# Reading the streamed operand of a matmul as two halves in turn, and the columns of all weight blocks 8 bytes apart

## Chip, cores and metric

The kernel runs on one core of a Trainium2 chip. The metric is the time of one execution on the device in microseconds (us). Before the change the median of three runs is 941.89 us, the lowest 941.58 us and the highest 941.97 us.

## What is computed

The reference is attention in a causal window of 128 positions with a linear bias per head, followed by a feed-forward block with a squared ReLU. There are 8 batches of 576 positions (4608 tokens), 8 heads of 64, a model width of 512 and a hidden width of 2048, all in float32.

```python
scores = scale * np.matmul(q, k.transpose(0, 1, 3, 2))
mask = (rel >= 0) & (rel < window)            # window = 128
scores = np.where(mask, scores + bias[None], -1000000000.0)
attn = np.exp(scores - np.max(scores, axis=-1, keepdims=True))
attn = attn / (np.sum(attn, axis=-1, keepdims=True) + 1e-09)
x = np.matmul(attn, v)                        # as (4608, 512)
h = np.maximum(x @ w_in, 0.0)                 # w_in (512, 2048)
return h * h @ w_out                          # w_out (2048, 512)
```

## The kernel before

**Tiling.** The 4608 tokens are cut into 9 chunks of 512 (`NCH`), the hidden width into 16 blocks of 128 (`NF`), the model width into 4 blocks of 128 (`NCC`). Everything in the feed-forward part is kept transposed: features lie on the 128 partitions, the 512 tokens of a chunk along each partition.

**The two products.** For each chunk `c` and hidden block `f`, `gemm1` (L194) makes one 128x512 result out of twelve matmuls (L202): four blocks `cc` of the model width, three matmuls each. `gemm2` (L223) adds to four 128x512 accumulators `acc`, one for each block `m` of the output, with three matmuls each (L231), twelve again. So each product has 9 x 16 x 12 = 1728 matmuls of 512 columns. Three matmuls stand for one float32 product: weight and data are each split into a high and a low part in a float32 type that TensorE takes in one pass (`F32R`, shown as fp32r or f32), and high times high, high times low and low times high are added. The streamed operands are `xs[cc][:, part]` (tile `xu`, part 0 high and part 1 low) in `gemm1`, and `hh` and `hl` in `gemm2`. Each is a row of 512 consecutive 4-byte words on every partition. Each matmul is recorded as two instructions: a weight load (LDWEIGHTS, engine PEld) of 128 columns, and the matmul itself (MATMUL, engine PE).

**Weights.** All weights stay in the on-chip memory. `weights_load` brings them in as pairs of 32-bit words (the inputs are float64, reinterpreted), and `convert` turns each pair in place into a low and a high part. So `self.w[f]` has the shape 128 x 2 x 512 x 2: product, column, low or high. `block` (L185) gives `gemm1` and `gemm2` the 128 columns of a block. Their words stand 8 bytes apart, since low and high alternate. For the blocks that `APART` (L39) picks, the host has stored the columns of two neighbouring blocks alternating, and `block` takes every second one, so that the words of one block stand 16 bytes apart. `APART` picks the first product alone, `f` = 0, 4, 8, 12, and of its four blocks the first two: six of the twelve weight loads of every fourth `gemm1`.

**Order.** TensorE's order is written out by hand. From chunk 1 on, the loop in `tile_attn_moe` alternates `gemm1` of step `n` with `gemm2` of step `n - 2`; once in eight such halves a `visit` puts the small matmuls of the attention (L541, L548) between them. Chunk 0 is ordered by a small planner with costs and due times (`Plan`, `start`), together with loads, weight conversion and the attention of the first chunks. Between the two products ScalarE and VectorE make `hh` and `hl` out of the result (L212 to L221). At the end of each chunk the four accumulators are copied out and written to the output, transposed; the host transposes it back.

Of the kernel before, what the change touches and what calls it, by code (L numbers as in the profile page):

```python
# [19 lines left out]
B, H, S, D = 8, 8, 576, 64  # L20
NP = H // 2
DM, DF = 512, 2048
NF = DF // 128
NCC = DM // 128
NCH = B * S // 512
# [10 lines left out]
GO = 20  # L36
SOON = (("z", 7),)
FIRST = 39
APART = lambda i, f, b: i == 0 and f % 4 == 0 and b < 2  # L39
CASTS = (0, 2, 15,)  # L40
COPIES = (3,)
SQUARES = (6,)
# [14 lines left out]

def slope(h):
    return 2.0 ** (-8.0 * (h + 1) / H)


class Kern:
# [120 lines left out]


    def block(self, i, f, b):  # L185

        w = self.w[f][:, i]
        if APART(i, f, b):
            w = w.rearrange("p (n j o) t -> p n o j t", n=2, o=2)[:, b // 2, b % 2]
        else:  # L190
            w = w[:, 128 * b : 128 * b + 128]
        return w[..., 0], w[..., 1]

    def gemm1(self, c, f):  # L194
        nc = self.nc
        xs = [self.x[c, p] for p in range(NP)]
        g = self.big.tile([128, 2, 512], F32, name="g")[:, 1] if self.big else self.g1.tile([128, 512], F32, name="g")
        i = 0
        for cc in range(NCC):
            wl, wh = self.block(0, f, cc)  # L200
            for w, part in ((wh, 0), (wh, 1), (wl, 0)):
                nc.tensor.matmul(g, w, xs[cc][:, part], start=i == 0, stop=i == 11)  # L202
                i += 1
                if (c, f, i) == (0, 0, 9):
                    yield
        yield
        r = self.hp.tile([128, 512], F32, name="r", bufs=1)
        hh = self.hp.tile([128, 512], F32R, name="hh")
        hl = self.hp.tile([128, 512], F32R, name="hl")
        self.h[c, f] = hh, hl  # L210
        with self.tc.high_priority(offset=100):
            self.relu = nc.scalar.activation(r, g, AF.Relu)  # L212
        yield
        if c or f in SQUARES:
            nc.vector.tensor_tensor(r, r, r, op=ALU.mult)  # L215
        else:
            nc.scalar.activation(r, r, AF.Square)
        yield
        nc.scalar.copy(hh, r)  # L219
        yield  # L220
        nc.vector.tensor_tensor(hl, r, hh.bitcast(F32), op=ALU.subtract)  # L221

    def gemm2(self, c, f):  # L223
        nc = self.nc
        hh, hl = self.h.pop((c, f))
        if f == 0:
            self.acc = self.start_banks if c == 0 else [self.ac.tile([128, 512], F32, name="acc") for _ in range(4)]
        for m in range(4):
            wl, wh = self.block(1, f, m)
            for i, (w, h) in enumerate(((wh, hh), (wh, hl), (wl, hh))):  # L230
                nc.tensor.matmul(  # L231
                    self.acc[m], w, h, start=(f == 0 and i == 0), stop=(f == NF - 1 and i == 2)
                )
            if f == NF - 1:
                o = self.op.tile([128, 512], F32, name="o")
                out = self.outd[m * 128 : m * 128 + 128, 512 * c : 512 * c + 512]
                (nc.scalar.copy if m % 2 else nc.vector.tensor_copy)(o, self.acc[m])
                (nc.scalar if c == NCH - 1 and m == 3 else nc.sync).dma_start(out, o)
# [598 lines left out]
def _consts():  # L837
    r = np.arange(128)
    own, h = r % 64, (r // 64)[:, None]
    cst = np.zeros((128, CST), np.float32)  # L840
    cst[:, 0:128] = np.eye(128)
    keep = own[:, None] >= np.arange(64)[None, :]
    cst[:, 128:192] = np.where(h == 0, keep, ~keep).astype(np.int32).view(np.float32)
    cst[:, 192:256] = NEG
    rel = r[:, None] - r[None, :]
    rel = np.where(rel >= 0, rel, rel + 128)
    for a in range(H):
        cst[:, 256 + 128 * a : 384 + 128 * a] = -rel * (8 * slope(a))
    later = r[:, None] < r[None, :]
    near = [cst[:, 256 + 128 * a : 384 + 128 * a] for a in range(H)]  # L850
    return np.concatenate([cst] + [np.where(late, t, np.float32(NEG)) for t in near for late in (later, ~later)], axis=1)


def _arrays(q, k, v, moe_w_in, moe_w_out):
    a = np.ascontiguousarray
    pairs = lambda x: x.transpose(1, 3, 0, 2).reshape(NP, 128, B * S)
    halo = lambda x: np.concatenate([np.zeros((NP, 128, 128), np.float32), x], axis=2)
    qt, kt = pairs(q), halo(pairs(k))
    qkd = np.stack([np.concatenate([
        qt[:, :, 512 * c : 512 * c + 256], kt[:, :, 512 * c : 512 * c + 640], qt[:, :, 512 * c + 256 : 512 * c + 512],  # L860
    ], axis=2) for c in range(NCH)])
    vt = np.zeros((NP, 1 + B * S // 128, 128, 128), np.float32)
    vt[:, 1:] = v.reshape(B, NP, 2, S, D).transpose(1, 0, 3, 2, 4).reshape(NP, B * S // 128, 128, 128)
    vd = np.stack([vt[:, 4 * c : 4 * c + 5].transpose(0, 2, 1, 3).reshape(NP, 128, 640) for c in range(NCH)])
    w1d = a(moe_w_in.reshape(NCC, 128, NF, 128).transpose(2, 1, 0, 3).reshape(NF, 128, NCC * 128))
    w2d = moe_w_out.reshape(NF, 128, DM).copy()
    for i, w in enumerate((w1d, w2d)):
        for f in range(NF):
            for n in range(2):
                if APART(i, f, 2 * n):  # L870
                    x = w[f, :, 256 * n : 256 * n + 256]
                    x[:] = x.reshape(128, 2, 128).transpose(0, 2, 1).reshape(128, 256).copy()
    return [a(qkd), a(vd), w1d.view(np.int64), w2d.view(np.int64), _consts()]


# [16 lines left out]
```

## Time and profile before

| what | value |
|---|---|
| median of three runs | 941.89 us |
| span of the profiled execution, first to last instruction | 939.1 us |
| L202 (first product), PE busy in the span | 423.89 us, 1728 matmuls |
| L231 (second product), PE busy in the span | 424.92 us, 1728 matmuls |
| PE busy, 0 to 35 us | 31.82 us |
| PE busy, 35 to 150 us | 112.80 of 115.00 us |
| PE busy, 300 to 700 us | 400.00 of 400.00 us |
| PE busy, 860 to 939.1 us | 75.38 of 79.10 us |

The profile was taken of one execution. Its page gives the span, from the first to the last instruction, and no separate device time for that execution; the device times of the three runs lie 2.5 to 2.9 us above the span. Records of matmuls overlap, since one starts streaming before the one ahead of it has drained; so the mean length of a record is no pace, and the pace is read from the distance between starts. PE is TensorE's matmuls, PEld its weight loads, which run beside them; DVE is VectorE, ACT is ScalarE.

### The profile page before, as it was taken

What the parts mean: (1) busy time and instruction counts of PE and PEld (TensorE: products, weight loads), DVE (VectorE), ACT (ScalarE), POOL (GpSimd) and SP (SyncE); (2) the same over time, 40 slices, a digit from 0 to 9 for tenths busy, and PEclk for the clock granted to TensorE, in tenths of its full rate; (3) what the DMA queues carried; (4) which work ended last, traced back from release to release, by engine and by line L of the source; (5) the groups of instructions that cost most, each with busy time, mean ns of one, the idle gap of its engine ahead of it and who ended that gap; (6) DMA issues with size and microseconds to landing.
All of it is one profiled execution on the core that took longest, in us unless ns stands there. A gap on an engine that the chain in (4) does not pass through costs nothing.

```text
span 939.1 us, 19485 instructions
## 1 busy us (share of the span) xinstructions
PE 929.3 (99%) x7492; PEld 782.5 (83%) x7492; DVE 497.2 (53%) x1326; ACT 418.9 (45%) x1115; POOL 214.2 (23%) x255
## 2 busy tenths in 40 slices
PE   8899999999999999999999999999999999999998
PEld 5688888888888888888888888888888888888886
DVE  5999874445554555544555444455455454433222
ACT  7898753343444444334434343344444444322222
POOL 4223331222221222222222222221221222220000
PEclk9999999999999999999999999999999999999999
DMA  9975424222432233222423233334322231111001
GB/s 344 403 284 167 135 74 130 71 62 83 129 86 85 78 104 107 64 84 79 125 86 86 73 106 82 86 85 127 88 77 83 75 93 43 38 46 45 1 0 45
DMA packets 72893, 95.26 MB, mean 101 GB/s; under 512 B 8032, under 2 KB 41952, under 8 KB 72800
## 3 DMA queue, kind: packets, MB, share of 16 engines
q1 hardware_dynamic: 72368, 93.36, 32.6%
q8 instruction: 59, 0.97, 0.4%
q10 hardware_dynamic: 432, 0.66, 0.2%
q14 instruction: 34, 0.28, 0.1%
HBM read 67.76 MB, written 26.21 MB: 100 GB/s over the span
## 4 chain that ended last, share of the span: by engine, by line
PE 94%; DMA 3%; DVE 1%; ACT 1%; issue 0%; SPq 0%; POOLq 0%; DVEq 0%
PE acc L231 43%; PE g L202 42%; PE s L541 5%; PE g L548 2%; DMA raw<-in_dram 2%; PE s L548 1%; DMA wide<-in_dram 1%; PE at L346 1%; ACT t L470 0%; PE s L412 0%; PE at L412 0%; DVE t L482 0%; DVE tw L613 0%; DVE pp L629 0%; DVE raw L175 0%
## 5 line engine op out<-in xcount | busy, mean ns | idle before, releaser
L202 PE MATMUL g<-xu,w 128*128 128x512 f32 x1728 | 423.9, 394 | 1.4 <-issue 0.8
L202 PEld LDWEIGHTS g<-xu,w 128*128 128x128 f32 x1728 | 344.6, 209 | 56.7 <-issue 1.7
L231 PE MATMUL acc<-hh,w 128*128 128x512 f32 x1152 | 385.6, 396 | 0.0
L231 PEld LDWEIGHTS acc<-hh,w 128*128 128x128 f32 x1152 | 224.0, 194 | 45.5 <-issue 5.3
L212 ACT ACTIVATE r<-g 128x512 f32<-128x512 f32 x144 | 86.1, 598 | 353.2 <-PE g L202 353.1
L215 DVE TENSOR_TENSOR r<-r 128x512 f32<-128x512 f32 x129 | 91.9, 713 | 255.8 <-ACT r L212 255.8
L231 PE MATMUL acc<-hl,w 128*128 128x512 f32 x576 | 226.2, 393 | 0.0
L334 POOL TENSOR_SCALAR_AFFINE_SELECT pp<-pp 128x512 f32<-128x512 f32 x128 | 112.5, 879 | 215.6 <-DMA pp<-way 139.4
L221 DVE TENSOR_TENSOR hl<-r,hh 128x512 fp32r<-128x512 f32 x144 | 117.6, 816 | 74.4 <-ACT hh L219 71.9
L270 POOL TENSOR_TENSOR t<-t,nm 128x512 f32<-128x512 f32 x64 | 76.1, 1190 | 262.0 <-DVE nm L267 231.4
L231 PEld LDWEIGHTS acc<-hl,w 128*128 128x128 f32 x576 | 112.1, 195 | 19.6
L219 ACT CAST hh<-r 128x512 fp32r<-128x512 f32 x144 | 89.2, 619 | 78.0 <-DVE r L215 76.4
L259 ACT ACTIVATE t<-t,nm 128x128 f32<-128x128 f32 x256 | 100.1, 394 | 11.8 <-DVE nm L252 11.7
L321 DVE STREAM_TRANSPOSE pp<-t 128x512 f32<-128x512 f32 x64 | 45.2, 707 | 47.0 <-POOL t L270 39.5
L252 DVE CUSTOM_DVE_ANT_0 t<-t,cst 128x128 f32<-128x128 f32 x256 | 59.5, 295 | 1.0
L541 PE MATMUL s<-pp,v 64*64 64x128 f32 (+1 forms) x1792 | 52.0, 248 | 0.1
L541 PEld LDWEIGHTS s<-pp,v 64*64 64x64 f32 x1792 | 40.5, 134 | 10.4 <-issue 10.0
L259 ACT ACTIVATION_READ_ACCUMULATOR t<-t,nm 128x1 f32 x256 | 48.6, 190 | 0.0
L482 DVE COPY_PREDICATED t<-cst,s 64x256 f32<-64x256 int32 x100 | 44.4, 444 | 6.0 <-ACT t L463 3.1
L472 POOL MEMSET t<- 64x128 f32 (+1 forms) x44 | 10.0, 228 | 117.8 <-PE s L548 110.5
L529 ACT CAST xu<-s 128x512 fp32r<-128x512 f32 x28 | 16.4, 587 | 41.6 <-DVE t L482 26.6
L470 ACT COPY t<-g 64x256 f32<-64x256 f32 (+2 forms) x86 | 28.0, 340 | 3.8 <-PE g L548 1.0
(71 smaller groups left out, 482.3 us busy)
## 6 DMA issues: line engine op xcount, KB each, us to landing
raw<-in_dram SPq DMA_DIRECT2D x32, 512.0 KB, 8.7
way<-pp SPq DMA_DIRECT2D x256, 64.0 KB, 2.0
pp<-way SPq DMA_DIRECT2D x64, 256.0 KB, 2.8
qk<-in_dram SPq DMA_DIRECT2D x32, 320.0 KB, 3.2
v<-in_dram SPq DMA_DIRECT2D x32, 320.0 KB, 3.9
qk<-in_dram SPq DMA_DIRECT2D x38, 256.0 KB, 4.3
out_dram<-o SPq DMA_DIRECT2D x35, 256.0 KB, 2.6
v<-in_dram SPq DMA_DIRECT2D x3, 256.0 KB, 5.2
```

The costliest lines, as they stand in the source:

```text
L202: nc.tensor.matmul(g, w, xs[cc][:, part], start=i == 0, stop=i == 11)
L212: self.relu = nc.scalar.activation(r, g, AF.Relu)
L215: nc.vector.tensor_tensor(r, r, r, op=ALU.mult)
L219: nc.scalar.copy(hh, r)
L221: nc.vector.tensor_tensor(hl, r, hh.bitcast(F32), op=ALU.subtract)
L231: nc.tensor.matmul(self.acc[m], w, h, start=(f == 0 and i == 0), stop=(f == NF - 1 and i == 2))
L252: self.nc.vector.tensor_tensor_reduce(self.t[:, m], self.t[:, m], self.K.nrel(2 * self.p + m // 2), -0.125, BIG, ALU.add, ALU.min, self.nm ...
L259: return self.nc.scalar.activation(self.t[:, m], self.t[:, m], AF.Exp, bias=nm[:, m : m + 1], scale=-1.0, accum_out=nm[:, 4 + m : 5 + m],)
L270: self.nc.gpsimd.tensor_tensor(self.t, self.t, self.nm[:, 8:12].unsqueeze(2).to_broadcast([128, 4, 128]), op=ALU.mult)
L321: nc.vector.transpose(squares.rearrange("p b m c -> p m b c"), self.t.rearrange("p m (b c) -> p m b c", c=32))
L334: nc.gpsimd.affine_select(to, self.own, pattern=[[-32 * sign, 4], [0, 4], [-sign, 32]], compare_op=op, fill=0.0, base=0, channel_multiplie ...
L541: made.append(mm(to, w, x, start=first and n < 2, stop=not first, skip_group_check=True))
```

## The change

The moving operand of all 3456 matmuls of the two products is read in another order. `in_turn` views a row of 512 words as two halves of 256 and runs over them in turn: word 0, word 256, word 1, word 257 and so on. Neighbouring words of the stream are then 1024 bytes apart, and the words of each half follow one another at every second place. The number of words, and the set of words, is as before.

`APART` is gone. Every weight block is 128 neighbouring columns, with words 8 bytes apart; the host stores the weights without the alternation.

As the stream's order sets the order of the result's columns, each product permutes the 512 tokens of a chunk once; the host puts them back with two permutations of the output.

Both edits change addresses alone: on every engine and queue the same instructions stand in the same order, with the same shapes.

```diff
-APART = lambda i, f, b: i == 0 and f % 4 == 0 and b < 2
...
+def in_turn(x):
+    return x.rearrange("p (a b) -> p b a", a=2)
...
     def block(self, i, f, b):
-
-        w = self.w[f][:, i]
-        if APART(i, f, b):
-            w = w.rearrange("p (n j o) t -> p n o j t", n=2, o=2)[:, b // 2, b % 2]
-        else:
-            w = w[:, 128 * b : 128 * b + 128]
+        w = self.w[f][:, i, 128 * b : 128 * b + 128]
         return w[..., 0], w[..., 1]
...
-                nc.tensor.matmul(g, w, xs[cc][:, part], start=i == 0, stop=i == 11)
+                nc.tensor.matmul(g, w, in_turn(xs[cc][:, part]), start=i == 0, stop=i == 11)
...
-                    self.acc[m], w, h, start=(f == 0 and i == 0), stop=(f == NF - 1 and i == 2)
+                    self.acc[m], w, in_turn(h), start=(f == 0 and i == 0), stop=(f == NF - 1 and i == 2)
...
-    w2d = moe_w_out.reshape(NF, 128, DM).copy()
-    for i, w in enumerate((w1d, w2d)):
-        for f in range(NF):
-            for n in range(2):
-                if APART(i, f, 2 * n):
-                    x = w[f, :, 256 * n : 256 * n + 256]
-                    x[:] = x.reshape(128, 2, 128).transpose(0, 2, 1).reshape(128, 256).copy()
-    return [a(qkd), a(vd), w1d.view(np.int64), w2d.view(np.int64), _consts()]
+    w2d = moe_w_out.reshape(NF, 128, DM)
+    return [a(qkd), a(vd), w1d.view(np.int64), a(w2d).view(np.int64), _consts()]
...
-    return np.ascontiguousarray(r.results[0]["out_0_dram"].T)
+    out = r.results[0]["out_0_dram"].T
+    for _ in range(2):
+        out = out.reshape(NCH, 256, 2, DM).transpose(0, 2, 1, 3).reshape(B * S, DM)
+    return np.ascontiguousarray(out)
```

## The prediction, made before the changed kernel ran

> **What bounds the kernel now.** I read the page's totals first, then its chain, then the groups of instructions, then TensorE's waits.
>
> ```profile
> span 939.1 us, 19485 instructions
> PE 929.3 (99%) x7492; PEld 782.5 (83%) x7492; DVE 497.2 (53%) x1326; ACT 418.9 (45%) x1115; POOL 214.2 (23%) x255
> PEclk9999999999999999999999999999999999999999
> PE acc L231 43%; PE g L202 42%; PE s L541 5%; PE g L548 2%; DMA raw<-in_dram 2%; PE s L548 1%; DMA wide<-in_dram 1%; PE at L346 1%; ACT t L470 0%; PE s L412 0%; PE at L412 0%; DVE t L482 0%; DVE tw L613 0%; DVE pp L629 0%; DVE raw L175 0%
> L202 PE MATMUL g<-xu,w 128*128 128x512 f32 x1728 | 423.9, 394 | 1.4 <-issue 0.8
> L231 PE MATMUL acc<-hh,w 128*128 128x512 f32 x1152 | 385.6, 396 | 0.0
> L231 PE MATMUL acc<-hl,w 128*128 128x512 f32 x576 | 226.2, 393 | 0.0
> ```
>
> TensorE is busy for 99% of the span, at the full granted clock in every slice. The chain that ended last runs through the two products for 43% and 42% of the span. They are 1728 + 1152 + 576 = 3456 matmuls of 512 columns, and before the first product TensorE waits 1.4 us in all. So each nanosecond that the change puts on a matmul's pace, or takes off it, counts 3456 times, and there is next to no slack that could swallow it. All other engines are busy half of the span or less.
>
> **The pace of a matmul now.** Records overlap, so I take it from a run of twelve on the timeline (start, length, and the count). The first row is a `gemm1` whose `f` is a multiple of 4, so with six weight loads at 16 bytes; the second is one without.
>
> ```profile
> 289.44 2.97 PE L202 MATMUL g<-xu,w 128*128 128x512 f32 x12
> 300.52 2.92 PE L202 MATMUL g<-xu,w 128*128 128x512 f32 x12
> 14.00 0.59 PE L129 MATMUL g<-zero 128*128 128x512 bf16 x2
> L129 PE MATMUL g<-zero 128*128 128x512 bf16 x2 | 0.6, 379 | 0.0
> ```
>
> Twelve matmuls have eleven distances and one last record of 0.39 us (the mean of 394 ns above). Without `APART` that is (2.92 - 0.39) / 11 = 0.230 us per matmul. With it the run is 2.97 - 2.92 = 0.05 us longer, 6 x 8 ns. The third and fourth rows show a stream of equally many columns, but 2-byte words, at full clock: 0.59 - 0.379 = 0.21 us from start to start, with the row's rounding up to 0.216. The 4-byte stream is thus 14 to 19 ns slower per 512 columns, although it has as many columns. Something that goes with bytes seems to hold it.
>
> **What a read costs by its step.** The change's own operation, a stream whose neighbouring words are far apart, stands nowhere in the trace: every matmul there streams consecutive words, or pieces of at least 32 of them. The nearest rows are weight loads, which read the same memory 128 words at a time with three steps. The first row is six loads at 16 bytes (in a window from 289.15 to 290.55 us), the second six at 8 bytes (from 300.25 to 301.6 us), the third loads of consecutive words in the attention, the fourth the same with 64 columns, the last all loads of the first product.
>
> ```profile
> L202 PEld LDWEIGHTS g<-xu,w 128*128 128x128 f32 x6 | 1.5, 309 | 0.0
> L202 PEld LDWEIGHTS g<-xu,w 128*128 128x128 f32 x6 | 1.2, 194 | 0.2
> L581 PEld LDWEIGHTS s<-qk 64*128 64x128 f32 x24 | 1.6, 186 | 2.5 <-DVE nm L591 1.6 <-DMA qk<-in_dram 0.9
> L541 PEld LDWEIGHTS s<-pp,v 64*64 64x64 f32 x1792 | 40.5, 134 | 10.4 <-issue 10.0
> L202 PEld LDWEIGHTS g<-xu,w 128*128 128x128 f32 x1728 | 344.6, 209 | 56.7 <-issue 1.7
> ```
>
> Sixty-four more columns of consecutive words cost 186 - 134 = 52 ns, so 128 columns take 104. From consecutive words to a step of 8 bytes the load grows by 8 ns, from 8 to 16 bytes by 115 ns. That fits a memory that hands out pieces of 16 bytes (my reading of the rows): 32, 64 and 128 pieces for the three loads, where the first is held by its columns (104 ns) and the others by their pieces. The price of a piece is then (309 - 194) / (128 - 64) = 1.80 ns. The stream of 512 consecutive 4-byte words takes 128 pieces, and 128 x 1.80 = 230 ns, which is just its measured pace; the 2-byte stream takes 64 pieces, 115 ns, and is held by its columns at 0.21 us instead. I take this agreement of two unlike operations as the strongest hint of the trace: the streams of the two products already run at the pace at which pieces arrive.
>
> **The change part by part.**
>
> *`APART` removed.* Six matmuls in every fourth `gemm1` lose about 8 ns each. There are 9 x 4 = 36 such runs: 36 x 0.05 = 1.8 us, and with a distance of 45 ns instead of the rounded 50 it is 1.6 us. All of it lies on TensorE's path. I take -1.6 us. If streams become much slower than loads, the loads at 16 bytes would have been hidden anyway and this gain is part of the rest; it never costs.
>
> *The streams in turn.* The cost per matmul lies between two ends. The lower end: a reader that keeps the piece of each half until its four words are used fetches 128 pieces as before, 0 ns; it could even lose the hold and come down to the 2-byte row's pace, about -14 to -19 ns. The upper end: a reader that fetches anew whenever the next word lies in another piece fetches 512 pieces, 512 x 1.80 = 920 ns per matmul, 690 ns more. The row nearest to the new stream is the weight load at 16 bytes, for it alone uses one word of a piece and goes on to another, and it pays the full 1.80 ns each time. It is not quite the same, since there the rest of the piece is never wanted, and here it is wanted two words later. I take the upper end: nothing in the trace shows that a reader holds more than the piece that it is on, and the price has been seen in two kinds of rows. So 3456 x 690 = 2385 us.
>
> What covers this? Nothing: TensorE is the engine that all wait for. The work of DVE, ACT and POOL per step stays, and gains slack. The DMA queues carry the same transfers and have more time. The rest of TensorE's time is not touched: 939.1 - 3456 x 0.230 = 144 us for the start, the attention's matmuls and the last copies. The waits inside the products are small, too, by TensorE's waits (waited for, us in all, times, longest):
>
> ```profile
> PE g L202 <- issue: 0.8, 1, 0.8
> PE g L202 <- DVE xu L530: 0.6, 1, 0.6
> ```
>
> A slower stream can at most swallow these 1.4 us.
>
> **The sum**, against the profiled execution: its span 939.1 - 1.6 + 2385 = 3322 us. The three runs have their median 2.8 us above the span (941.89 against 939.1), and the page gives the profiled execution no other time of its own; with the same 2.8 us the kernel takes **3325 us**. If a piece costs less, down to the 0.21 to 0.216 us of the 2-byte stream over 128 pieces (1.69 ns), the stream has 864 ns, 634 more, and the time is 942 + 2191 = 3133 us. If it costs (230 + 8) / 128 = 1.86 ns, as the pace beside loads at 16 bytes would have it, 952 ns and 942 + 2495 = 3437 us. So this case by itself spans 3130 to 3440.
>
> **The rivals.**
>
> *Both pieces are held.* The reader (or a buffer ahead of it) keeps one piece of each half, and the order of the words doesn't matter, only the number of different pieces, still 128. What speaks for it: both the load rows and the matmul's pace count different pieces, and no row shows a piece fetched twice; in the load at 16 bytes twice as many bytes are truly touched. Against it: nothing shows such a buffer. Then only `APART` counts, 941.89 - 1.6 = **940.3 us**, 0.17% less, just inside the 0.2% that I count as no change, since a measurement of this kernel can hardly tell less. If the 36 runs lose 50 ns and their borders a little more, it is over 0.2% (940.0). It decides from the point at which two pieces fit; there is no step between. I give it 0.31, of it 0.20 inside 0.2% and 0.11 over.
> [...]
>
> *Two streams that overlap.* If fetches from two far places run side by side, the hold on the 4-byte stream goes, and each matmul comes down from 230 to some 215 ns: say -15 x 3456 = -52 us, with `APART` 941.9 - 52 - 1.6 = **888 us**. It speaks for it that the stream is now slower than its columns need; against it, that no two reads of one operand overlap in any row. This is the rival that ends clearly on the other side; it needs all 3456 streams to be held by the wait for a piece and not by its transfer. 0.07.
>
> *A factor of two.* Words come in pairs, and a pair from two pieces is fetched at once, or each extra fetch costs no more than the columns themselves: 256 x 1.80 = 460 ns, 230 more, 795 us in all: 941.9 + 795 - 1.6 = **1735 us**. For it: the load at 16 bytes, too, grew by about the time of its columns (115 ns, against 104 for 128 columns) and no more. Against it: then the 4-byte stream's 230 ns would need another reason. 0.14. Between it and the forecast lies a price that is added to each word, 0.9 ns (115 / 128) on top of 0.45 ns (230 / 512): 1.35 x 512 = 690 ns, 460 more, some 2530 us. 0.06.
> [...]
>
> **How the numbers follow.** The forecast, 512 pieces at 1.80 ns, gets 0.42; a factor of two 0.14; the price in between 0.06; both pieces held 0.31; overlapping streams 0.07. Slower by over 0.2%: 0.42 + 0.14 + 0.06 = 0.62. Within 0.2%: 0.20. Faster by over 0.2%: 0.11 + 0.07 = 0.18. The range leaves out only the overlap (0.07), since without "both held" too much would be missing: from 936 us (940.3 and some us for matmuls that gain a little) to 3440 us. It is wide because the cases lie far apart; between 950 and 1700 I expect nothing. The likeliest case's own range is 3130 to 3440.
>
> **What would show it.** In the changed kernel's profile the run of twelve at L200 (now L202) gives the pace at once: 0.92 us for the forecast, 0.46 or 0.69 for the cases between, 0.23 if both pieces are held, 0.21 to 0.216 for the overlap. The weight loads of L200 should have a mean of 194 instead of 209 ns in every case, and in every run of twelve alike. With a pace of 0.92 the shares of the chain must be 47 to 48% for each product, and DVE's busy share fall to some 15% with the same busy time of about 497 us. The forecast is wrong if the pace stays at 0.23, for then the order of words within the touched pieces costs nothing; the size is wrong if the pace is a multiple of 0.23 other than four.

## The result, and the profile after

The changed kernel takes **899.5 us** (median of four runs, 899.3 to 899.6) against 941.74 us (four runs of the kernel before, 940.76 to 941.97): a ratio of 0.9556, interval 0.9543 to 0.957. It is faster by 42 us, where the prediction had 3325 us and slower. The page of the changed kernel, with the rows that answer to those shown of before:

```profile
span 897.9 us, 19481 instructions
PE 880.7 (98%) x7488; PEld 782.1 (87%) x7492; DVE 504.1 (56%) x1326; ACT 426.6 (48%) x1115; POOL 209.3 (23%) x255
PE 87%; DVE 5%; ACT 3%; DMA 3%; issue 1%; SPq 0%; DVEq 0%; ACTq 0%; POOLq 0%
L200 PE MATMUL g<-xu,w 128*128 128x512 f32 x1728 | 400.4, 381 | 7.5 <-ACT r L210 4.3
L200 PEld LDWEIGHTS g<-xu,w 128*128 128x128 f32 x1728 | 340.3, 198 | 44.6 <-ACT r L210 5.5
L229 PE MATMUL acc<-hh,w 128*128 128x512 f32 x1152 | 369.3, 382 | 0.0
```

The busy time of the first product falls from 423.9 to 400.4 us. At the same time two things are worse than before: TensorE waits 7.5 us ahead of the first product instead of 1.4, and the chain that ended last, which was TensorE's for 94% of the span, now runs through it for 87%, and through VectorE and ScalarE for 8%. Its row of before reads

```profile
PE 94%; DMA 3%; DVE 1%; ACT 1%; issue 0%; SPq 0%; POOLq 0%; DVEq 0%
```

The chain of one execution is a weak sign, though: e12_near5 below, which has lost nothing in chunk 0, has 89%.

The pace stands in the timeline: a run of twelve matmuls of the first product, and the start of the second product behind it.

```profile
308.50 2.75 PE L200 MATMUL g<-xu,w 128*128 128x512 f32 x12
311.09 0.38 PE L229 MATMUL acc<-hh,w 128*128 128x512 f32 x1
```

From 308.50 to 311.09 are twelve distances: 2.59 / 12 = 0.216 us per matmul, against 0.230 before. That is the pace of the 2-byte stream in the kernel before (0.215 to 0.216 us for the pair shown there; other such pairs of its trace start 0.226 apart): the 4-byte stream has lost its hold. 3456 matmuls at 14.3 ns less (230.1 to 215.8; for each run of twelve from chunk 1 on the mean of its eleven distances, and of these means the median) are 49 us, and 42 were gained. Where the rest went is seen when the kernel is cut at chunk 1. These are the first matmuls of chunk 1 and the last of all, first of the kernel before:

```profile
138.15 1.11 PE L202 MATMUL g<-xu,w 128*128 128x512 f32 x4
...
934.99 0.39 PE L231 MATMUL acc<-hh,w 128*128 128x512 f32 x1
```

and of the changed kernel:

```profile
141.77 1.03 PE L200 MATMUL g<-xu,w 128*128 128x512 f32 x4
...
893.64 0.38 PE L229 MATMUL acc<-hh,w 128*128 128x512 f32 x1
```

Chunks 1 to 8 went from 934.99 - 138.15 = 796.8 to 893.64 - 141.77 = 751.9 us: 45 us, as the pace says (8 x 384 x 14.3 ns = 43.9, and 1.4 from the weight blocks). But chunk 0, with 384 matmuls that are 14 ns faster too, ends 3.6 us *later* instead of 5.5 earlier. Some 9 us are given back there.

Why is chunk 0 later? In its time the weights are converted. The groups from 35 to 120 us on ScalarE and VectorE, before:

```profile
L179 ACT CAST w<-raw 128x1024 fp32r<-128x1024 f32 x13 | 15.0, 1160 | 3.8 <-DVE raw L177 3.6
L219 ACT CAST hh<-r 128x512 fp32r<-128x512 f32 x13 | 8.1, 622 | 0.4
L177 DVE SCALAR_TENSOR_TENSOR raw<-raw 128x1024 int32<-128x1024 int32 x14 | 19.2, 1369 | 0.2
```

and after:

```profile
L182 ACT CAST w<-raw 128x1024 fp32r<-128x1024 f32 x12 | 18.8, 1575 | 4.8 <-DVE raw L180 4.7
L217 ACT CAST hh<-r 128x512 fp32r<-128x512 f32 x12 | 7.4, 618 | 0.3
L180 DVE SCALAR_TENSOR_TENSOR raw<-raw 128x1024 int32<-128x1024 int32 x13 | 20.8, 1599 | 0.2
```

The same steps on the weights, whose words stand 8 bytes apart, take 1575 instead of 1160 ns on ScalarE and 1599 instead of 1369 on VectorE. The cast of `hh`, on consecutive words, takes 618 ns as before. TensorE then waits for ScalarE. The timeline row of the longest such wait, and the window behind it (from and to, length, busy time and count of PE, PEld, DVE, ACT and POOL, granted clock, share of the DMA engines, GB/s):

```profile
87.34 4.46 PE L200 MATMUL g<-xu,w 128*128 128x512 f32 x12 [2.38 <-ACT r L210]
87.20:90.60 3.40, 3.26 (x8) 2.64 (x9) 3.23 (x5) 3.34 (x5) 0.00 (x0) 0.50 0.35 74
```

After the wait of 2.38 us the granted clock is 0.50 for 3.4 us, and the run takes 4.46 us instead of 2.75. But the 9 us do not hang on the clock. With two places 256 bytes apart (e15_d256 below) the same run, after a wait almost as long, stays at clock 1.00,

```profile
87.45 2.87 PE L200 MATMUL g<-xu,w 128*128 128x512 f32 x12 [2.24 <-ACT r L210]
```

and chunk 1 begins at 141.8 us all the same.

### The profile page after: what moved, and what is told of

It is laid out like the page before. It is cut to its first block, busy times and chain, and to the rows that moved or that the text cites. A ratio compares the mean times of both kernels' runs of the same rounds, so it can differ in the third digit from the quotient of the medians.

```text
span 897.9 us, 19481 instructions
## 1 busy us (share of the span) xinstructions
PE 880.7 (98%) x7488; PEld 782.1 (87%) x7492; DVE 504.1 (56%) x1326; ACT 426.6 (48%) x1115; POOL 209.3 (23%) x255
## 4 chain that ended last, share of the span: by engine, by line
PE 87%; DVE 5%; ACT 3%; DMA 3%; issue 1%; SPq 0%; DVEq 0%; ACTq 0%; POOLq 0%
PE acc L229 39%; PE g L200 38%; PE s L539 5%; PE g L546 2%; DMA raw<-in_dram 2%; PE s L546 1%; DVE raw L180 1%; ACT raw L176 1%; DMA wide<-in_dram 1%; DVE w L184 1%; ACT t L468 1%; DVE raw L178 1%; ACT t L257 1%; DVE t L480 0%; PE at L344 0%
## 5 line engine op out<-in xcount | busy, mean ns | idle before, releaser
L200 PE MATMUL g<-xu,w 128*128 128x512 f32 x1728 | 400.4, 381 | 7.5 <-ACT r L210 4.3
L200 PEld LDWEIGHTS g<-xu,w 128*128 128x128 f32 x1728 | 340.3, 198 | 44.6 <-ACT r L210 5.5
L229 PE MATMUL acc<-hh,w 128*128 128x512 f32 x1152 | 369.3, 382 | 0.0
L229 PEld LDWEIGHTS acc<-hh,w 128*128 128x128 f32 x1152 | 226.4, 196 | 26.6 <-issue 5.3
L229 PE MATMUL acc<-hl,w 128*128 128x512 f32 x576 | 218.3, 379 | 0.0
L213 DVE TENSOR_TENSOR r<-r 128x512 f32<-128x512 f32 x129 | 88.2, 684 | 226.6 <-ACT r L210 226.3
L219 DVE TENSOR_TENSOR hl<-r,hh 128x512 fp32r<-128x512 f32 x144 | 121.3, 843 | 75.5 <-ACT hh L217 75.5
L268 POOL TENSOR_TENSOR t<-t,nm 128x512 f32<-128x512 f32 x64 | 70.6, 1105 | 254.8 <-DVE nm L265 240.3
```

What stands on the lines that cost most here:

```text
L200: nc.tensor.matmul(g, w, in_turn(xs[cc][:, part]), start=i == 0, stop=i == 11)
L229: nc.tensor.matmul(self.acc[m], w, in_turn(h), start=(f == 0 and i == 0), stop=(f == NF - 1 and i == 2))
L268: self.nc.gpsimd.tensor_tensor(self.t, self.t, self.nm[:, 8:12].unsqueeze(2).to_broadcast([128, 4, 128]), op=ALU.mult)
```

## Experiments

All kernels below start from the changed one, with the weight blocks 8 bytes apart, and differ in the order in which `in_turn` reads the 512 words (and in the host's permutation that undoes it), unless a diff says otherwise. Each ran once, unless a number of runs is given. Paces are, as above, the median over the runs of twelve, chunks 1 to 8, of a run's mean distance from start to start. A **piece** is, as in the prediction's reading of the load rows, 16 aligned bytes, four words; what the runs say of its size is worked out below.

### Whole pieces, pairs, quarters, neighbours

```diff
 def in_turn(x):
-    return x.rearrange("p (a b) -> p b a", a=2)
+    return x.rearrange("p (a n b) -> p n a b", a=2, b=4)   # e1_quads; b=2: e2_pairs
+    return x.rearrange("p (a b) -> p b a", a=4)            # e3_quarters
+    return x.rearrange("p (n a b) -> p n b a", a=2, b=4)   # e4_near
```

> The streams go over the two halves four words at a time: words 0 to 3, 256 to 259, 4 to 7 and so on, so that every 16-byte piece is read whole and neighbouring pieces of the stream lie 1 KB apart. Four theories of why the changed kernel's pace fell from 230 to 216 ns. TWO READERS (every second word goes to another reader, each keeps one piece): each reader needs 128 pieces again, pace 230 ns, time about 940 us. FAR PLACES (fetches overlap when the next piece lies far away): 216 ns, about 900 us. SAME PIECE (one piece gives out words slower than the array takes them, and another piece in between hides it): 3 of 4 steps stay in the piece, so near 230 ns, about 930 to 940 us. CLASH (the 14 ns come from the weight loads beside the stream, and depend on the stream's order only through where it reads): no firm number, between 216 and 230 ns.

> The streams go over the two halves two words at a time: words 0, 1, 256, 257, 2, 3 and so on. TWO READERS: each reader jumps at every word and needs 256 pieces, 256 x 1.80 = 460 ns, about 1735 us. FAR PLACES: 216 ns, about 900 us. SAME PIECE: half of the steps leave the piece, about 223 ns, about 920 us.

> The streams go over four quarters in turn, word by word: words 0, 128, 256, 384, 1 and so on. TWO READERS: each jumps at every word, 460 ns, about 1735 us. FAR PLACES and SAME PIECE: 216 ns as with two halves, about 900 us, if four pieces can be kept; if only two can, every word is a new fetch and the pace is 460 to 920 ns.

> The streams go in turn over two neighbouring pieces of 16 bytes: words 0, 4, 1, 5, 2, 6, 3, 7, then 8, 12 and so on. TWO READERS: 64 pieces for each, 216 ns, about 900 us. FAR PLACES: the pieces are neighbours, so 230 ns, about 940 us. SAME PIECE: 216 ns, about 900 us.

| kernel | pace, ns | time, us | kernel before beside it |
|---|---|---|---|
| e1_quads | 247 | 1003.38 | 940.94 |
| e2_pairs | 327 | 1277.52 | 940.94 |
| e3_quarters | 273 | 1087.02 | 940.94 |
| e4_near | 216 | 893.28 | 940.94 |

In e1_quads and e3_quarters the rows read

```profile
307.61 3.20 PE L200 MATMUL g<-xu,w 128*128 128x512 f32 x12
310.64 0.42 PE L229 MATMUL acc<-hh,w 128*128 128x512 f32 x1
```

```profile
305.21 3.44 PE L200 MATMUL g<-xu,w 128*128 128x512 f32 x12
308.50 0.44 PE L229 MATMUL acc<-hh,w 128*128 128x512 f32 x1
```

with (310.64 - 307.61) / 12 = 0.253 and 0.274 us. The first run is one of the slower ones of e1_quads: 28 of its 128 runs in the first product have 253 ns, and nearly all others 247; what divides them is open.

FAR PLACES falls: reading far apart, piece by piece, is slower than consecutive words (247), and neighbouring pieces in turn give the full gain. SAME PIECE falls: with half or all steps leaving the piece, pairs and quarters are slower still (it had 223 and 216). TWO READERS has the order right (64, 128 and 256 pieces for each reader: 216; 247; 273 and 327), but it had 230 for the second, and 460 ns for the last two is far too much. And neighbouring pieces are better than the change itself.

### The parts of the change, the weight loads, chunk 0

```diff
-                nc.tensor.matmul(g, w, in_turn(xs[cc][:, part]), start=i == 0, stop=i == 11)
+                nc.tensor.matmul(g, w, xs[cc][:, part], start=i == 0, stop=i == 11)     # e5_straight, e7_packed
+                nc.tensor.matmul(g, w, in_turn(xs[cc][:, part]) if c else xs[cc][:, part], start=i == 0, stop=i == 11)  # e8_later
...
-        w = self.w[f][:, i, 128 * b : 128 * b + 128]
-        return w[..., 0], w[..., 1]
+        w = self.w[f][:, i].rearrange("p d t -> p (d t)")                                # e7_packed
+        return w[:, 256 * b : 256 * b + 128], w[:, 256 * b + 128 : 256 * b + 256]
```

The second product is edited in the same way. e6_kept is the kernel before, with `APART`, and the streams in turn.

> The change without its streams in turn: only the weight blocks at 16 bytes are gone, the streams read consecutive words. All theories: 36 runs of twelve lose some 45 ns, 1.6 us, so about 940.1 us against 941.7 (0.9983); pace 230 ns everywhere. If more than 5 us are gained here, the gain of the change does not come from the streams.

> The streams in turn with the weight blocks of before, 216 loads at 16 bytes. If a load at 16 bytes takes 128 pieces of 1.80 ns, 230 ns, it is now longer than a stream of 216 ns and sets the pace of its matmul: 230 to 238 ns for six of twelve in every fourth first product, 36 x 6 x 14 to 22 ns = 3 to 5 us, about 903 us against 899.5. If the load's 115 ns are mere delay and not occupancy, the pace stays at 216 ns and the time at 899.5 us.

> Streams of consecutive words, and weight loads of consecutive words too: the blocks are taken out of the weights as 128 neighbouring words, low and high parts mixed, so the products are others than the reference's. The loads take 32 pieces instead of 64. CLASH: with half of the load's fetches the stream loses half of its 14 ns or all of it, pace 216 to 223 ns. TWO READERS and SAME PIECE: the stream is held by its own reads, 230 ns as before, about 940 us. Loads about 186 ns in every case.

> The streams in turn from chunk 1 on, consecutive in chunk 0. In the changed kernel chunk 0 came out later (chunk 1 starts at 141.8 us against 138.1 before), with the weight conversion's steps on ScalarE and VectorE longer beside the streams in turn: 1.5 to 1.8 us where they took 1.15 to 1.25. If the streams in turn slow them, chunk 0 is as before here (chunk 1 starts at 138 us, steps at 1.15 to 1.25 us) and the time is about 896 us. If the steps are longer for another reason, chunk 1 starts at 141 to 142 us or later and the time is 899.5 us or more.

**e5_straight**: 940.76 us (ten runs) against 941.58, ratio 0.9994, interval 0.9985 to 1.0004. The 36 runs lost their longer pace, but what that is worth, at most 1.6 us, is below what the measurement tells from nothing. So the gain is the streams'.

**e6_kept**: 904.15 us (four runs), ratio 0.961 (0.9594 to 0.9626), 4.65 us above the changed kernel. A run with six loads at 16 bytes now reads

```profile
309.14 2.88 PE L206 MATMUL g<-xu,w 128*128 128x512 f32 x12
311.85 0.38 PE L235 MATMUL acc<-hh,w 128*128 128x512 f32 x1
```

2.71 us for the twelve, 0.12 more than 2.59, 36 times: 4.3 us. The matmuls beside these loads have paces of 235 to 240 ns. In the kernel before it was no other: its run from 289.44 us ends where the next product starts, at 292.24, which leaves (2.80 - 6 x 0.230) / 6 = 0.237 us for each of the six. So a load at 16 bytes occupies something for about that long, and what was worth hardly anything with a stream of 230 ns is worth 4.65 us with one of 216: the two edits are not a sum of two.

**e7_packed**: loads of 188 ns and 32 pieces, and a pace of 233.5 ns (948.57 us), not less than 230. CLASH, which had 216 to 223, falls, and that leaves the stream's own reads for the hold. Why the pace is 3.5 ns longer with these loads was not found.

**e8_later**: 896.4 us (four runs), ratio 0.9525 (0.951 to 0.9539), 3.1 us better than the changed kernel. Chunk 1 starts at 138.0 us, ScalarE's cast of the weights has a mean of 1154 ns from 35 to 120 us. So it is the streams in turn, 1 KB apart, that lengthen the conversion.

### What a reader is

> The streams read first all even words, then all odd ones: words 0, 2, 4 ... 510, 1, 3 ... . TWO READERS (every second word of the stream goes to another reader, each keeps one piece): each reader finds one word in a piece and needs 256 pieces, as with pairs and with quarters, which took 327 and 273 ns; so 273 to 327 ns, 1085 to 1280 us. ONE READER that keeps the piece it is on: 256 pieces in all, two words each, twice the 128 of consecutive words: 460 ns at 1.80 ns for a piece, 1735 us. ALTERNATION (only neighbours of the stream in one piece are slow to come): half of the steps stay in a piece, 216 to 230 ns, 900 to 940 us.

> The streams go over four neighbouring pieces in turn, word by word: words 0, 4, 8, 12, 1, 5, 9, 13 and so on. TWO READERS with one piece each: each jumps at every word, 256 pieces, so 273 ns as with four quarters, about 1085 us, or somewhat less if nearness helps. Readers that keep two pieces each, or ALTERNATION: 216 ns, about 893 us, and then the 273 ns of four far quarters are owed to the distance and not to the jumps.

> The streams read every fourth word: 0, 4, 8 ... 508, then 1, 5, 9 and so on, one word of each piece. MEETING (two readers, and a fetch is dear only when both want the same piece at the same time, as with consecutive words, pairs and even words): neighbours of the stream are in different pieces, so about 270 ns as with four pieces or four quarters in turn, about 1075 us. ONE READER (each new piece costs 1.77 to 1.80 ns, as the even words' 453 ns and the weight loads at 16 bytes have it): 512 pieces, 906 to 920 ns, about 3280 us; but then four quarters in turn should have cost as much.

> The streams read every eighth word: 0, 8, 16 and so on, each 32 bytes from the one before. MEETING: 270 ns as with every fourth word. If neighbouring pieces lie in two banks of the memory, every eighth word stays in one bank for 64 words, and the pace is up to twice that of every fourth word.

```diff
+    return x.rearrange("p (b a) -> p a b", a=2)            # e9_step2; a=4: e13_step4; a=8: e14_step8
+    return x.rearrange("p (n a b) -> p n b a", a=4, b=4)   # e10_qnear
```

Even words, then odd (e9_step2, 1707.78 us), and every fourth word (e13_step4, 1737.78 us):

```profile
309.96 5.62 PE L200 MATMUL g<-xu,w 128*128 128x512 f32 x12
315.40 0.63 PE L229 MATMUL acc<-hh,w 128*128 128x512 f32 x1
```

```profile
314.37 5.73 PE L200 MATMUL g<-xu,w 128*128 128x512 f32 x12
319.91 0.64 PE L229 MATMUL acc<-hh,w 128*128 128x512 f32 x1
```

(315.40 - 309.96) / 12 = 0.453 and 5.54 / 12 = 0.462 us. Every eighth word (1632.03 us) has 432 ns, four neighbouring pieces in turn (1071.61 us) 269 ns. Staying at every second piece (every eighth word) makes nothing slower, so no two banks of neighbouring pieces show.

For the even words ALTERNATION (216 to 230 ns) falls, TWO READERS at the price of pairs and quarters (273 to 327) missed as well, and the 453 ns are what ONE READER had (460). Every fourth word tells these apart.

The first two settle most of it. With every fourth word each of the 512 words is a new piece; with even words only every second one is. They cost the same. **One reader** with a price for each new piece can't do that: 0.90 ns a piece, which fits every fourth word (512 x 0.90 = 461), would give the even words 230 and consecutive words 115. MEETING falls too: it had 270 ns for every fourth word. **Two readers**, each taking every second word of the stream, fit, if each new piece costs its reader 1.80 ns (a sum made after these runs, not before): with every second, fourth or eighth word each needs 256 pieces, and 256 x 1.80 ns, the price from the weight loads of the kernel before, is 460 ns (453, 462, 432 measured). Consecutive words: both readers go through all 128 pieces, 230 ns (230). Two pieces in turn: each reader reads its own run, 64 pieces, 115 ns, so by this sum the pieces hold the stream no longer, and it has the pace of the 2-byte stream of as many columns (216 ns against 215 to 216 for the pair shown before); that this is the time of the columns themselves is not shown. In this picture the size of a piece comes out too: with pieces of 8 bytes consecutive words would cost as much as even words (230 and 453 were measured), and with 32 bytes even words half of every fourth word (453 and 462).

Three orders don't fit this price: pairs (327), far and near quarters (273, 269) have jumps at every word of a reader, but each reader comes back to the piece it left two words before. They lie between the 230 ns of 128 fetches and the 460 of 256, so in this picture something of a piece that was left is still there on return, and how much is open. With whole far pieces (247 against 230) a jump seems to cost some more by itself. That there are two readers, rather than one that takes two words at a time in some other way, is a picture that fits the paces; no run looks inside.

### How far apart, and the best version

```diff
-    return x.rearrange("p (a b) -> p b a", a=2)
+    return x.rearrange("p (n a b) -> p n b a", a=2, b=16)  # e11_d64; b=64: e15_d256; b=128: e16_d512; b=4: e12_near5
```

> The streams go over two runs of 16 words in turn, 64 bytes apart: words 0, 16, 1, 17 and so on. TWO READERS: 64 pieces each, 216 ns. On the weight conversion's steps beside it in chunk 0 (1150 to 1400 ns with consecutive words and with pieces 16 bytes apart, 1420 to 1720 with halves 1 KB apart): if only pieces at the same place of some larger grid, 1 KB apart, collide with the other engines, they are as short as with neighbouring pieces, and the time is about 893 us; if any two places that are not neighbours do, the steps are long and the time is about 899 us.

> Two runs in turn 256 bytes apart. Pace 216 ns. If the weight conversion's steps in chunk 0 are as short as at 16 and 64 bytes, about 891 to 893 us; if they are long as at 1 KB, about 899 us.

> Two runs in turn 512 bytes apart. Pace 216 ns. If the steps in chunk 0 are long at 1 KB alone, they are short here and the time is 891 to 893 us; if from 512 bytes on, about 899 us.

> Two neighbouring pieces in turn once more, against the kernel before in five rounds: 893.3 us in one run, so a ratio of 0.949 to 0.950, below the changed kernel's 0.9556 and below that of halves in turn from chunk 1 on (0.9525).

| apart | pace, ns | time, us | first matmul of chunk 1, us |
|---|---|---|---|
| 16 bytes (e12_near5, five runs; the same kernel as e4_near) | 216 | 891.75 | 134.0 |
| 64 bytes (e11_d64) | 216 | 891.22 | 133.3 |
| 256 bytes (e15_d256) | 216 | 899.86 | 141.8 |
| 512 bytes (e16_d512) | 216 | 899.52 | 141.6 |
| 1024 bytes (the change, four runs) | 216 | 899.5 | 141.8 |

A run of twelve at 16 bytes takes 313.63 - 311.04 = 2.59 us, as in the change:

```profile
311.04 2.75 PE L200 MATMUL g<-xu,w 128*128 128x512 f32 x12
313.63 0.38 PE L229 MATMUL acc<-hh,w 128*128 128x512 f32 x1
```

The pace doesn't know the distance; chunk 0 does. ScalarE's two conversion steps from 35 to 120 us at 16 bytes,

```profile
L182 ACT CAST w<-raw 128x1024 fp32r<-128x1024 f32 x13 | 14.9, 1158 | 4.1 <-DVE raw L180 3.9
L176 ACT ACTIVATE raw<-raw 128x1024 f32<-128x1024 f32 x13 | 14.6, 1159 | 0.1
```

and at 512 bytes:

```profile
L182 ACT CAST w<-raw 128x1024 fp32r<-128x1024 f32 x12 | 18.8, 1595 | 4.9 <-DVE raw L180 4.8
L176 ACT ACTIVATE raw<-raw 128x1024 f32<-128x1024 f32 x13 | 18.5, 1457 | 0.0
```

So the second loss hangs on the distance, with a border between 64 and 256 bytes (the cast has a mean of 1166 ns at 64 bytes and of 1608 at 256). 16 bytes apart is the best with several runs (64 bytes had 891.22 us in its one): **891.75 us**, ratio 0.9479 (0.9466 to 0.9492), a little below the 0.949 to 0.950 expected. From the first matmul of chunk 1 to the last it is as fast as the change; the 7.75 us between them are the 7.8 us of chunk 0 (141.8 - 134.0). Why two far places lengthen the other engines' steps was not found. Number of fetches alone it is not: quarters, with more jumps, left the cast at 1182 ns, but at a slower pace of the stream; whole far pieces lengthened it to 1679 ns.

## Why the prediction was wrong

- **What bounds the kernel** was right: TensorE's pace times 3456. So was the reading that the 4-byte stream is held at 230 ns by something else than its number of columns: as many columns take 216 ns in another order. That the hold is pieces at 1.80 ns is not shown as it was meant, with one reader: 512 new pieces (e13) cost 462 ns and not 920. It fits if two readers share the stream. The price itself rests on the loads at 8 and 16 bytes. The step before it, 52 ns for 64 more columns, passed over a row: the loads of the transposes (L622), 128 consecutive words too, have a mean of 140 ns, not 186.
- **The step that failed** is "I take the upper end: nothing in the trace shows that a reader holds more than the piece that it is on". It took the weight load at 16 bytes as the nearest row and multiplied 512 words by 1.80 ns. In that row the rest of a piece is never wanted; in the change it is wanted two words later, as the prediction itself noted. The run shows 216 ns instead of 920. Even the order that makes all 512 words new pieces (e13) takes 462: half of the price assumed, as if two fetches went on side by side.
- **The lower end** of the cost was right: "it could even lose the hold and come down to the 2-byte row's pace". The rival "two streams that overlap", with 0.07, had this pace and 888 us. Its condition was not the right one: distance does not decide, as e1 (far, and slower) and e4 (near, and as fast) show; the number of pieces per reader fits. So its closeness is in part luck. It missed 11 us: some 9 in chunk 0, and 2.4 because it took 15 ns where 14.3 were gained.
- **`APART`** was put at -1.6 us by itself. Alone it is 0.8 us, within the measurement (e5). In the change it is worth 4.65 us (e6): the prediction weighed streams that become longer than these loads and hide them, and they became shorter. The mean of the loads at L200 came down to 198 ns, where it had 194.
- **"What covers this? Nothing"** and "the work of DVE, ACT and POOL per step stays" were wrong for chunk 0: the conversion steps became up to 415 ns longer (1160 to 1575), and chunk 0 gave back some 9 us; a version without the longer steps is 7.75 us faster (e12).
- **The range**, 936 to 3440 us, left out the one case that came. All that the trace showed was that the 4-byte streams were slower than a 2-byte stream of as many columns (230 against 215 to 226 ns); that is an opening for a gain as much as a warning of a loss, and 0.07 was too little for it.

## What to carry to other kernels

When a stream of 4-byte words is slower than a 2-byte stream of as many columns (here 230 against 215 to 226 ns), look at the order in which its words come before giving it up: two neighbouring pieces in turn took 14 ns of 230 off every matmul here, at no cost in instructions, with a permutation of the output as the only price. A price read from an operation that never returns to what it left behind was not the price for one that does (920 ns by the loads' 1.80 ns a piece, 216 measured); measure it with one kernel, since the ends here lay a factor of four apart. And when one engine's reads change, look again at the length of the other engines' instructions beside it (ScalarE's cast went from 1160 to 1575 ns here), not only at their order.

## What had not been expected of the hardware

- Streams of 512 four-byte words: 230 ns in consecutive order, 216 with two pieces in turn at each of five distances from 16 to 1024 bytes, 247 to 327 with jumps every few words, 432 to 462 with every second, fourth or eighth word.
- A weight load of 128 columns took 186, 194 and 309 ns at steps of 4, 8 and 16 bytes (140 at 4 bytes in the transposes), and the last sets a pace of 235 to 240 ns, beside streams of 216 ns and of 230 alike.
- Beside streams with two places far apart, ScalarE's cast of words 8 bytes apart took 1608, 1595 and 1575 ns at 256, 512 and 1024 bytes, against 1160 before, and VectorE's step on them 1683 and 1599 at 512 and 1024, against 1369; ScalarE's cast of consecutive words had 622 before and 638, 618 and 618. At 16 and 64 bytes the cast of words 8 bytes apart took 1158 and 1166 ns, VectorE's step 1334 and 1363.
- After a wait of 2.38 us, in a stretch with several, TensorE's granted clock was 0.50 for 3.4 us; after waits of 2.24 and 2.20 us at the same place (e15, e16) it stayed at 1.00.
